# Where the raw weight pieces of a fused attention, Fourier and feed-forward kernel lie, and when the last of them are converted

## The chip, the cores and the metric

The kernel runs on one core of a Trainium2 chip. The core has five engines that run side by side and each take their own instructions strictly in order: TensorE (PE, with its weight loads as PEld), VectorE (DVE), ScalarE (ACT), GpSimd (POOL) and SyncE (SP), which here only issues DMAs. The metric is the device time of one execution in microseconds; lower is better.

## The reference

For 4 sequences of 768 tokens and 8 heads of 64 features, queries and keys are each given to one of 16 clusters, and a query attends only to keys of its own cluster. The heads are laid side by side (512 features), a two-dimensional Fourier transform is taken over tokens and features, its real part is added, and a normalised two-layer feed-forward net follows.

```python
mask = q_assign[:, :, :, None] == k_assign[:, :, None, :]
scores = np.where(mask, scale * np.matmul(q, k.transpose(0, 1, 3, 2)), -1000000000.0)
...
X = np.fft.fft(np.fft.fft(x, axis=1), axis=2)
u = x + np.real(X).astype(np.float32)
...
un = (u - mu) / np.sqrt(var + 1e-06)
ch = np.maximum(un @ w_ch1, 0.0) @ w_ch2
return (u + ch).astype(np.float32)
```

The two weight matrices (512 x 2048 and 2048 x 512) arrive as 64-bit floats. The kernel turns each into a pair of 16-bit matrices (a high and a low half) on the chip.

## The kernel before, in words

**Steps.** `Overlap.run` writes the order of the work out by hand. The attention has 16 pairs of heads, each with 6 blocks of 128 queries; one block of one pair is one step. Step 5 scores the first block, step 100 the last; steps 5 to 28 are pairs 0 to 3, which make up the first sequence. In each step `Attention.scores` runs 16 matmuls (L320, L325), VectorE reduces the two score tiles to their maxima (L339, result `rmx`, kept in `att.late`), ScalarE takes exponentials (L342) and rounds them to 16 bits (L350), GpSimd subtracts to get the low half (L351), and SyncE issues a DMA transpose per head (L353, tile `pt`). Two or three steps later `Attention.attend` multiplies with the values (L371 to L373). `prep` loads and splits the queries and keys of the next pairs (L210, L216, L236). While pairs 0 to 3 are scored, the exponentials lie in the tile `X[1]`, which nothing else needs yet.

**Weights.** `Weights.run` is a generator that is called once per conversion step k, beside the attention. The 2 x 16 pieces of 128 x 512 values are numbered 0 to 31: 0 to 15 are the first layer's, 16 to 31 the second's. `load` fetches a piece raw (512 KB, L481). `signs` (L506, L507, ScalarE, two pieces per instruction) picks the exponent bits of the piece into a sign image; `block` (L491, 8 matmuls per 4 pieces, then L494 and L58 to L61 on VectorE) finds the scale of four pieces; `join` (L515 on PE, L519 on VectorE) makes the 32-bit value in PSUM; `halve` writes the high half (L525, ScalarE) and the low half: an even piece by one VectorE instruction (L531), an odd one by a ScalarE copy and a GpSimd subtraction (L528, L529). `relative` (L563 to L569) closes the conversion with small VectorE instructions.

Raw pieces and sign images lie in the `Arena`, 48192 bytes per partition that later hold the transform's and the feed-forward net's activations. There are eight raw places (`RAW`), so the load of piece p waits until piece p - 8 has been joined. Conversion step i is called at attention step 0.684 i: the first join stands ahead of step 5, the last one behind the scores of step 25.

**What follows.** At step 31 `Fourier.fold` folds the first sequence (L641, L642, halves in L625 and L626, two DMA transposes L648); from step 32 the transform's matmuls (L697, L712) and, from step 36, the feed-forward net's (L842, L873) are interleaved with the attention of the next sequence. Only PE's order is taken as written; on the other engines a scheduler places instructions by its own estimate of when they are ready.

## Time and profile before

| what | value |
|---|---|
| runs | 1043.43 us median of 3 (1041.61 to 1048.4) |
| the profiled execution | 1042.51 us, its span 1040.7 us |
| mean granted PE clock | 0.951 |
| busy in the span | PE 916.0 us, DVE 607.9, ACT 604.3, POOL 588.1 |
| read from HBM | 42.52 MB |

The profile's views used below are: the table of stretches (busy time of each engine between two moments, with the number of instructions, the granted clock and the DMA share, which can pass 1 because it is the packets' time over the time of 16 engines); the groups of instructions by line and shape; the timeline of one engine; and the list of waits (which engine waited at which line for which). A step is timed from its first L339 instruction on VectorE to the next step's.

### The profile page before, as it was taken

To read this page: it belongs to the slowest core of one execution; us is meant where nothing else is said; L and a number is where in the kernel's file an instruction comes from. 1 tells how busy PE (TensorE), PEld (TensorE's weight loads), DVE (VectorE), ACT (ScalarE), POOL (GpSimd) and SP (SyncE) were. 2 spreads that over 40 slices of the span, in tenths; PEclk is the share of its full clock that TensorE was granted. 3 is DMA by queue.
4 is the path that set the end of the run, shared out by engine and by line. 5 is a ranking of instruction groups with operands and counts; after the bars stand their busy time and mean duration, and the time that the engine had idled before them with its cause. 6 is when DMAs were issued, how large, how long until landed. Compare 5 with 4: busy or idle time off the path is not lost.

```text
span 1040.7 us, 23567 instructions
## 1 busy us (share of the span) xinstructions
PE 916.0 (88%) x9396; PEld 592.0 (57%) x9416; DVE 607.9 (58%) x1264; ACT 604.3 (58%) x948; POOL 588.1 (57%) x694
## 2 busy tenths in 40 slices
PE   4776676667999999998999999997999999899998
PEld 2243343444765757554756758555757676586683
DVE  6788789778555555668656555577555423621110
ACT  5899897645755656454756747455666552342230
POOL 2466577556766756636857747448857553362230
PEclk9588978879999999998999999998999999999999
DMA  7799998977668676679667767488656561411000
GB/s 266 197 252 242 276 208 188 180 145 147 146 104 178 104 148 143 121 143 171 114 134 148 139 123 148 92 149 176 115 108 128 96 125 32 81 42 31 11 11 21
DMA packets 396239, 140.01 MB, mean 135 GB/s; under 512 B 381784, under 2 KB 381792, under 8 KB 396128
## 3 DMA queue, kind: packets, MB, share of 16 engines
q1 hardware_dynamic: 396128, 138.50, 65.1%
q8 instruction: 73, 1.20, 0.5%
q14 instruction: 38, 0.31, 0.1%
HBM read 42.52 MB, written 6.29 MB: 47 GB/s over the span
## 4 chain that ended last, share of the span: by engine, by line
PE 43%; DVE 14%; DMA 9%; POOL 9%; ACT 7%; issue 7%; SPq 1%; ACTq 0%; POOLq 0%; DVEq 0%
PE ps_f L873 17%; PE ps_f L842 15%; PE ps_big L320 4%; DMA pt<-ph 4%; POOL ph L351 3%; DVE ps_big L339 3%; ACT ph L350 2%; DMA scr<-in_k_dram 2%; DMA arena<-arena 1%; PE ps_o L371 1%; ACT p L342 1%; PE ps_f L697 1%; PE ps_o L372 1%; PE ps_o L373 1%; DVE X L339 1%
## 5 line engine op out<-in xcount | busy, mean ns | idle before, releaser
L351 POOL TENSOR_TENSOR ph<-p,ph 128x768 f16<-128x768 f32 x144 | 241.8, 1687 | 181.3 <-ACT ph L350 149.0
L842 PE MATMUL ps_f<-arena,w1h 128*128 128x256 f16 x1536 | 271.1, 276 | 22.5 <-ACT arena L851 9.5
L873 PE MATMUL ps_f<-w2h,arena 128*128 128x512 f16 x768 | 239.0, 379 | 0.5 <-ACT arena L851 0.5
L842 PE MATMUL ps_f<-arena,w1l 128*128 128x256 f16 x768 | 211.9, 276 | 0.0
L342 ACT ACTIVATE p<-ps_big,rmx 128x768 f32<-128x768 f32 x144 | 128.9, 900 | 133.8 <-DVE ps_big L339 120.3
L873 PEld LDWEIGHTS <-arena 128*128 128x128 f16 x1152 | 108.7, 98 | 127.2 <-issue 5.8
L842 PEld LDWEIGHTS <-w1h 128*128 128x128 f16 x1536 | 151.9, 99 | 36.7 <-issue 12.7
L852 POOL TENSOR_TENSOR arena<-arena 128x256 f16<-128x256 f32 x192 | 128.6, 680 | 74.5 <-ACT arena L851 70.4
L339 DVE TENSOR_SCALAR_CACHE_REDUCE ps_big<-ps_big,sce 128x768 f32<-128x768 f32 x144 | 141.4, 1020 | 44.2 <-PE ps_big L325 44.2
L320 PE MATMUL ps_big<-hlk,hlq 64*128 64x384 f16 x1152 | 127.7, 346 | 36.2 <-ACT p L342 22.1
L873 PE MATMUL ps_f<-w2l,arena 128*128 128x512 f16 x384 | 145.5, 379 | 0.0
L371 PE MATMUL ps_o<-v,pt 128*128 128x66 f16 x1152 | 121.8, 197 | 14.5 <-DVE X L387 7.4
L851 ACT ACTIVATE arena<-ps_f,wrel 128x256 f16<-128x256 f32 x192 | 90.6, 474 | 70.9 <-DVE arena L848 69.2
L350 ACT CAST ph<-p 128x768 f16<-128x768 f32 x144 | 117.9, 832 | 15.9 <-DMA pt<-ph 15.3
L848 DVE TENSOR_SCALAR arena<-ps_f,wrel 128x256 f32<-128x256 f32 x96 | 46.2, 481 | 136.4 <-POOL arena L852 82.1
L371 PEld LDWEIGHTS <-pt 128*128 128x128 f16 x1152 | 108.6, 99 | 27.6 <-issue 16.8
L372 PE MATMUL ps_o<-v,pt 128*128 128x64 f16 x1152 | 121.7, 197 | 0.0
L373 PE MATMUL ps_o<-v,pt 128*128 128x66 f16 x1152 | 121.2, 196 | 0.0
L372 PEld LDWEIGHTS <-pt 128*128 128x128 f16 x1152 | 109.2, 99 | 2.7
L320 PEld LDWEIGHTS <-hlq 64*128 64x128 f16 x1152 | 55.0, 98 | 96.0 <-issue 64.8
L373 PEld LDWEIGHTS <-pt 128*128 128x128 f16 x1152 | 109.4, 101 | 0.0
L842 PEld LDWEIGHTS <-w1l 128*128 128x128 f16 x768 | 75.9, 99 | 23.3 <-issue 14.2
(176 smaller groups left out, 1328.9 us busy)
## 6 DMA issues: line engine op xcount, KB each, us to landing
arena<-in_moe_w_ch_dram SPq DMA_DIRECT2D x32, 512.0 KB
scr<-in_q_dram SPq DMA_DIRECT2D x16, 384.0 KB
scr<-in_k_dram SPq DMA_DIRECT2D x16, 384.0 KB
vst<-in_v_dram SPq DMA_DIRECT2D x16, 384.0 KB
out_dram<-arena SPq DMA_DIRECT2D x24, 256.0 KB
pt<-ph SPq DMA_TRANSPOSE x168
arena<-in_cs_dram SPq DMA_DIRECT2D x12, 192.0 KB
arena<-in_ss_dram SPq DMA_DIRECT2D x12, 192.0 KB
```

Source lines behind the costliest of these rows:

```text
L320: nc.tensor.matmul(out=ps[j][:, hf, 0:SH], lhsT=hq[rows[j], a, sl], rhs=hk[rows[j], c, hs], start=(i == 0), stop=False)
L339: self.mark = nc.vector.tensor_scalar(out=ju, in0=ps[j][:, :, 0:SH], scalar1=ne, scalar2=None, op0=ALU.mult, op1=ALU.min, accum_out=m)
L342: nc.scalar.activation(x, ju, AF.Exp, bias=m, scale=-1.0)
L350: nc.scalar.copy(out=ph[:, 0], in_=p32)
L351: nc.gpsimd.tensor_tensor(out=ph[:, 1], in0=p32, in1=ph[:, 0], op=ALU.subtract)
L371: nc.tensor.matmul(out=o[:, at:at + W], lhsT=hi, rhs=v16[:, kt, 0:W], start=(kt == 0), stop=False)
L372: nc.tensor.matmul(out=o[:, at:at + D], lhsT=hi, rhs=v16[:, kt, 66:130], start=False, stop=False)
L373: nc.tensor.matmul(out=o[:, at:at + W], lhsT=lo, rhs=v16[:, kt, 0:W], start=False, stop=(kt == ST - 1))
L842: nc.tensor.matmul(out=ps.rearrange("p (t x) -> p t x", x=P), lhsT=a[:, dc, fs], rhs=c[:, :, dc], start=(i == 0), stop=(i == 11))
L851: nc.scalar.activation(hh[:, f], ps, AF.Relu, scale=rel[:, f:f + 1])
L852: nc.gpsimd.tensor_tensor(out=hl[:, f], in0=r, in1=hh[:, f], op=ALU.subtract)
L873: nc.tensor.matmul(out=ps, lhsT=a[:, f, ts], rhs=c[:, f], start=(i == 0), stop=(i == 47))
```

## The change

Three things move. (1) The arena is laid out anew: two of the eight raw places, the small tables `ID`, `TOP`, `MX`, `ONE` and `X32` change their offsets, and the transform's table `CD` starts 32 bytes later. (2) Pieces 8 to 15 are loaded into the space of the second layer's halves (`w2h`, `w2l`), which are written only from piece 16 on, so 16 raw pieces can be held at once. For pieces 8 to 23 GpSimd first copies one column of `att.late` into the raw place (L484), and the load waits for that copy: it can't start before the scores of the step in which it is written. (3) Pieces 24 to 31 get raw places and sign images of their own (`RAWB`, `PNB`), which lie in the first 20.5 KB of the arena and near its end, where the feed-forward net's activations come later, so that they can still be converted while `fold` and the transform use the rest; two images lie in parts of `X` (`spare`).

With these, the conversion's pace changes: from step 8 of the generator on it is called every 0.85 attention steps instead of every 0.684. The loads follow a table (`TIMES`), `signs` is called one place earlier, the signs of pieces 8 to 15 and 24 to 31 take two instructions of 512 values each instead of sharing two of 1024, and the odd pieces from 25 on make their low half on VectorE.

```diff
+    RAW, PN = tuple(4128 * i for i in range(6)) + (28864, 32992), (24768, 39168, 43264)
+    LAST = 24
+    RAWB, PNB = (0, 4104, 8208, 12312), (16416, 18464, 45216)
+    EXTRA, AHEAD, THR = 8, 7, 1
+    TIMES = {8: 1, 9: 1, 10: 2, 11: 3, 12: 4, 13: 4, 14: 5, 15: 6, 16: 7, 17: 8, 18: 10, 19: 11, 20: 13, 21: 14, 22: 16, 23: 17,
+             24: 18, 25: 19, 26: 20, 27: 21, 28: 25, 29: 26, 30: 27, 31: 28}
...
+        self.spare = X[0][:, 2:6, 3 * P:DM].bitcast(BF16), X[1][:, 4:6, DM // 2:DM].bitcast(BF16)
...
     def raw(self, k):
-        n, e = len(self.RAW), self.EXTRA
-        if n <= k < n + e:
-            o = 16 * DM - 2064 * ((k - n) // 2 + 1)
-            return self.w2[k % 2].rearrange("p a x -> p (a x)")[:, o:o + 4 * DM + 8].bitcast(U16)
-        return self.arena.at(self.RAW[(k if k < n else k - e) % n], [P, 4 * DM + 8], U16)
+        n = len(self.RAW)
+        if n <= k < n + self.EXTRA:
+            return self.w2x[k % 2][:, 4 * DM * ((k - n) // 2):][:, 0:4 * DM + 2].bitcast(U16)
+        at = self.RAW[k % n] if k < self.LAST else self.RAWB[(k - self.LAST) % len(self.RAWB)]
+        return self.arena.at(at, [P, 4 * DM + 2], U16)
...
     def load(self, k):
+        if len(self.RAW) <= k < self.LAST and self.att.late is not None and self.THR:
+            self.nc.gpsimd.tensor_copy(out=raw[:, 2:4].bitcast(F32), in_=self.att.late)
...
     def signs(self, k):
+        if k >= self.LAST or n <= k < n + self.EXTRA:
+            for i in range(k, k + 2):
+                if k < self.LAST:
+                    b = at(self.PN[k // 2 % 3], [P, 2, 2, DM], BF16)[:, :, i % 2]
+                else:
+                    b = at(self.PNB[i % 4], [P, 2, DM], BF16) if i % 4 < 3 else self.spare[i // 4 % 2]
+                self.bits[i] = b
+                top = self.raw(i)[:, 4:4 + 4 * DM - 3:4]
+                for j, t in enumerate((top.bitcast(I16), top)):
...
+                    nc.scalar.activation(o, t, AF.Relu, bias=self.off[:, j:j + 1], scale=8.0)
+            return
...
-        if k % 2:
+        if k % 2 and k < self.LAST:
             x = self.arena.at(self.X32, [P, DM], F32)
...
-            if k % 2 == 0 and 0 <= k + 2 < 32:
+            if k == self.LAST + 4:
+                self.signs(k + 2)
+                yield
+            if k == self.LAST + 2:
                 self.signs(k + 2)
...
+            if k % 2 and 0 <= k + 3 < self.LAST + 4:
+                self.signs(k + 3)
...
-    W0, WD = 0, 0.684
+    W0, WD, WE = 0, 0.684, 0.85
...
-        n = 32 + self.wts.AHEAD + 2
+        n = 32 + self.wts.AHEAD + 3
         for i in range(n):
-            at(int(self.W0 + i * self.WD), 6, weights, None)
+            at(int(self.W0 + i * self.WD) if i < 8 else int(T0 + (i - 7.3) * self.WE), 6, weights, None)
```

Joins per stretch of steps, counted from the two built programs: ahead of step 5 one in both; steps 5 to 21, 25 before and 20 now; steps 22 to 28, 6 and 7; steps 29 to 32, none and 4. The block of pieces 28 to 31 and `relative` stand behind step 28 now. From step 32 on PE's order is the same in both. The changed file is 31 lines longer, so its lines bear higher numbers: L519 becomes L544 (join), L531 becomes L556 (low half), L494 becomes L500 (block), L641, L642 and L626 become L671, L672 and L656 (fold), L481 becomes L487 (load).

The first place is VectorE from the maximum of the values of a later pair (L248) through the fold of the first sequence, steps 31 and 32. Before:

```order
L641 TENSOR_TENSOR arena<-X_63 128x1536
L248 TENSOR_REDUCE amx<-vst 128x1
L339 TENSOR_SCALAR ps_big,rmx<-ps_big,sce 128x2x384 x2
L201 SCALAR_TENSOR_TENSOR v_2831<-vst,scp,v_2831 128x6x64
L626 SCALAR_TENSOR_TENSOR arena<-arena,vseq 128x768
L641 TENSOR_TENSOR arena<-X_63 128x1536
L642 TENSOR_TENSOR arena<-arena 128x3x255
L626 SCALAR_TENSOR_TENSOR arena<-arena,vseq 128x768
L339 TENSOR_SCALAR ps_big,rmx<-ps_big,sce 128x2x384 x2
```

The same place in the changed kernel:

```order
L556 SCALAR_TENSOR_TENSOR w2l<-ps_f,wsc,w2h 128x512
L248 TENSOR_REDUCE amx<-vst 128x1
L339 TENSOR_SCALAR ps_big,rmx<-ps_big,sce 128x2x384 x2
L201 SCALAR_TENSOR_TENSOR v_2840<-vst,scp,v_2840 128x6x64
L656 SCALAR_TENSOR_TENSOR arena<-arena,vseq 128x768
L671 TENSOR_TENSOR arena<-X_63 128x1536
L544 SCALAR_TENSOR_TENSOR ps_f<-arena,ps_f 128x512 x2
L672 TENSOR_TENSOR arena<-arena 128x3x255
L556 SCALAR_TENSOR_TENSOR w2l<-ps_f,wsc,w2h 128x512 x2
L339 TENSOR_SCALAR ps_big,rmx<-ps_big,sce 128x2x384 x2
L201 SCALAR_TENSOR_TENSOR v_3014<-vst,scp,v_3014 128x6x64
L656 SCALAR_TENSOR_TENSOR arena<-arena,vseq 128x768
```

Five conversion instructions now stand inside the fold, and the second halving of the fold (L626, now L656) has moved behind the two maxima of step 32 and a value split.

The second place is the DMA queue, SP, from the transposes of step 6 to those of step 8 (`ph` and `p` are the two heads' tiles of one step). Before:

```order
L353 DMA_TRANSPOSE pt<-ph 128x12x128
L353 DMA_TRANSPOSE pt<-p_357 128x12x128
L481 DMA arena<-in_moe_w_ch_dram 128x2048
L353 DMA_TRANSPOSE pt<-ph 128x12x128
L353 DMA_TRANSPOSE pt<-p_411 128x12x128
L481 DMA arena<-in_moe_w_ch_dram 128x2048 x2
L353 DMA_TRANSPOSE pt<-ph 128x12x128
L481 DMA arena<-in_moe_w_ch_dram 128x2048
L353 DMA_TRANSPOSE pt<-p_492 128x12x128
L303 DMA_TRANSPOSE oht<-oh 128x9x128
L481 DMA arena<-in_moe_w_ch_dram 128x2048 x2
```

In the changed kernel:

```order
L353 DMA_TRANSPOSE pt<-ph 128x12x128
L353 DMA_TRANSPOSE pt<-p_362 128x12x128
L487 DMA w2l<-in_moe_w_ch_dram 128x2048
L353 DMA_TRANSPOSE pt<-ph 128x12x128
L353 DMA_TRANSPOSE pt<-p_408 128x12x128
L487 DMA w2h<-in_moe_w_ch_dram 128x2048
L487 DMA w2l<-in_moe_w_ch_dram 128x2048
L487 DMA w2h<-in_moe_w_ch_dram 128x2048
L353 DMA_TRANSPOSE pt<-ph 128x12x128
L353 DMA_TRANSPOSE pt<-p_474 128x12x128
L487 DMA w2l<-in_moe_w_ch_dram 128x2048
L303 DMA_TRANSPOSE oht<-oh 128x9x128
```

The loads of pieces 12, 13 and 14 now stand in a row ahead of the transposes of step 8, where two loads stood.

## The prediction

> **What bounds the kernel now.** I read the page's slices first, then the table of stretches cut at attention steps, then the groups of instructions in these stretches, and last VectorE's timeline where the first sequence is folded.

> ```profile
> span 1040.7 us, 23567 instructions
> PE   4776676667999999998999999997999999899998
> DVE  6788789778555555668656555577555423621110
> ACT  5899897645755656454756747455666552342230
> 260.00:860.00 600.00, 568.82 (x6265) 377.24 (x6264) 352.71 (x728) 355.86 (x574) 378.62 (x435) 0.99 0.70 133
> ```

> A slice is 26 us. From the eleventh on PE is at 9 nearly everywhere, and it is busy for 568.82 of the 600 us from 260 on: there the matmuls set the pace, and whatever comes late before 260 us is handed on to the end. In the first ten slices PE is at 4 to 7, and VectorE and ScalarE at 6 to 9. This first quarter is the part that the change touches. The steps in it are bounded by VectorE's first maximum of each:

> ```profile
> 28.79 1.01 DVE L339 TENSOR_SCALAR_CACHE_REDUCE X<-ps_big,sce 128x768 f32<-128x768 f32 x1
> 145.86 1.02 DVE L339 TENSOR_SCALAR_CACHE_REDUCE X<-ps_big,sce 128x768 f32<-128x768 f32 x1
> 191.54 1.02 DVE L339 TENSOR_SCALAR_CACHE_REDUCE ps_big<-ps_big,sce 128x768 f32<-128x768 f32 x1
> 221.58 1.01 DVE L339 TENSOR_SCALAR_CACHE_REDUCE ps_big<-ps_big,sce 128x768 f32<-128x768 f32 x1
> ```

> These are steps 5, 22, 29 and 32. Cut there, the stretches read (time, PE, PE loads, VectorE, ScalarE, GpSimd busy, then clock, DMA share, GB/s):

> ```profile
> 28.80:145.90 117.10, 83.67 (x932) 45.40 (x947) 97.98 (x202) 107.17 (x139) 71.42 (x63) 0.83 1.06 242
> 145.90:191.50 45.60, 30.96 (x404) 19.43 (x409) 38.42 (x85) 35.90 (x49) 31.32 (x27) 0.81 0.86 173
> 191.50:221.60 30.10, 16.70 (x211) 10.38 (x208) 22.62 (x29) 15.32 (x20) 19.35 (x14) 0.72 0.86 160
> 221.60:258.20 36.60, 28.92 (x329) 18.71 (x327) 28.64 (x67) 21.44 (x35) 20.93 (x23) 0.92 0.78 159
> ```

> Steps 5 to 21 take 6.9 us each with 25 joins among them, steps 22 to 28 take 6.5 us with 6. ScalarE is busy 0.915 of the first stretch and 0.787 of the second; the DMA share falls from 1.06 to 0.86; VectorE alone has the same share in both, 0.837 and 0.843. So the conversion fills ScalarE and the DMA engines early, and VectorE is as full as it gets all along. No single engine is the bound; ScalarE and VectorE feed each other in order.

> **The change part by part.** *Steps 5 to 28* (28.8 to 191.5, 162.7 us). The prices:

> ```profile
> L519 DVE SCALAR_TENSOR_TENSOR ps_f<-arena,ps_f 128x512 uint32<-128x512 uint32 x31 | 21.0, 685 | 0.7 <-ACT ph L350 0.5 <-PE ps_f L515 0.2
> L531 DVE SCALAR_TENSOR_TENSOR w2l<-ps_f,wsc,w2h 128x512 f16<-128x512 f32 x8 | 5.9, 742 | 1.7 <-ACT w2h L525 1.7
> L494 DVE TENSOR_REDUCE arena<-ps_f 128x1 f32<-128x512 f32 x7 | 4.8, 681 | 0.8 <-PE ps_f L491 0.8
> L59 DVE TENSOR_SCALAR ps_f<-ps_f 128x1 int32<-128x1 int32 x7 | 1.1, 161 | 0.1
> L566 DVE TENSOR_SCALAR wrel<-arena 128x16 f32<-128x16 f32 x1 | 0.5, 504 | 0.0
> L506 ACT ACTIVATE arena<-arena 128x1024 int16<-128x1024 int16 x13 | 15.9, 1224 | 4.6 <-PE ps_f L491 3.3 <-DMA arena<-in_moe_w_ch_dram 1.2
> L525 ACT ACTIVATE w2h<-ps_f,wsc 128x512 f16<-128x512 f32 x16 | 10.9, 688 | 1.4 <-DVE ps_f L519 1.4
> L528 ACT ACTIVATE arena<-ps_f,wsc 128x512 f32<-128x512 f32 x16 | 11.0, 685 | 0.0
> L529 POOL TENSOR_TENSOR w2l<-arena,w2h 128x512 f16<-128x512 f32 x4 | 4.6, 1160 | 9.5 <-ACT arena L528 9.5
> ```

> VectorE loses 4 joins (2.74 us), one block (0.68 and four small instructions of about 0.16, together 1.32) and `relative` (0.50 and four small ones, 1.1). Its low halves stay 15: pieces 28 and 30 leave, 25 and one more odd piece come in. That is 5.2 us less: from 97.98 + 38.42 = 136.4 to 131.2 us. At the steady share of 0.838 the stretch would take 156.5 us, a gain of 6.2. ScalarE loses 4 high halves and 4 copies (8 x 0.686 = 5.5). Its sign instructions go from 24 of 1024 values (29.4 us) to 8 of those and 30 of 512. No such short one is in the trace; its price lies between half of 1.22 (0.61) and the 512-value instruction L525 (0.69), so 28.1 to 30.5 us in all. I take the upper end, since L525 is as long and the nearest row: ScalarE goes from 143.07 to about 138.7 us, which at its share over the stretch, 0.879, is 157.7 us, a gain of 5.0. The DMA engines gain nothing here: all pieces from 8 on are still loaded between steps 5 and 28. I take 5.5 us, between the two engines that feed each other. At the one end stands no gain, if the transfers set the pace; at the other 11 us, if the whole stretch ran at ScalarE's early share of 0.915 (138.7 / 0.915 = 151.6).

> *The waits of the loads.* GpSimd gets 16 copies like that which already guards the loads of the values:

> ```profile
> L189 POOL COPY vst<-rmx x14: 177/187/198, 38.6 to 711.2; 128x1 f32<-128x1 f32 x14
> POOL vst L189 <- DVE X L339: 3.7, 1, 3.7
> ```

> They are 3.0 us against the 4 subtractions of 1.16 that it loses, and GpSimd is busy 102.7 of 162.7 us, so I cost them at nothing; without that cover 3.0. Each waits for the second maximum of a step, and behind it on GpSimd stands the subtraction (L351) of that step or the next, for which the transposes wait. That subtraction waits for an exponential and a rounding behind the first maximum anyway, which end later, so the copy is the later of the two only in single places; the one such wait in this stretch took 3.7 us.

> *Steps 29 to 31.* Here nothing was converted, and now four pieces are: on VectorE 4 joins, 4 low halves, a block and `relative`, 2.74 + 2.97 + 1.32 + 1.1 = 8.1 us, in a stretch where it was busy 22.62 of 30.1. Where the rest was:

> ```profile
> 200.96 0.95 DVE L216 TENSOR_REDUCE amx<-scr 128x1 f32<-128x768 f32 x1 [4.51 <-DMA scr<-in_q_dram]
> 203.00 1.02 DVE L339 TENSOR_SCALAR_CACHE_REDUCE ps_big<-ps_big,sce 128x768 f32<-128x768 f32 x1
> 215.28 1.76 DVE L641 TENSOR_TENSOR arena<-X 128x1536 f32<-128x1536 f32 x1
> 217.07 2.27 DVE L642 TENSOR_TENSOR arena<-arena 128x765 f32<-128x765 f32 x1
> 220.35 1.31 DVE L626 SCALAR_TENSOR_TENSOR arena<-arena,vseq 128x768 f16<-128x768 f32 x1 [1.00 <-ACT arena L625]
> 223.45 0.61 DVE L201 SCALAR_TENSOR_TENSOR v<-vst,scp,v 128x384 f16<-128x384 f32 x1
> 218.58 3.64 PE L697 MATMUL ps_f<-arena 128*128 128x257 f16 x18 [0.56 <-DMA arena<-arena]
> 227.69 1.20 PE L697 MATMUL ps_f<-arena 128*128 128x257 f16 x6
> ```

> The one long gap, 4.51 us before step 30, is a wait for a load of queries; the block, the join of piece 28 and `relative` now stand ahead of it or just in it, and can fill it. What is left, 8.1 - 4.5 = 3.6 us, falls into steps 30 and 31, where VectorE runs from 203.00 to 221.58 with little idle: five conversion instructions stand inside the fold. The fold's second halving feeds the even matmuls that began at 227.69, and PE takes everything in order, so I let all 3.6 us through. Bounds: 0.6, if all 7.5 idle us are filled, and 10.6, if none is and the halving also waits for the two maxima and the value split that now stand ahead of it (from 221.58 to 223.45, and 0.61: 2.5).

> [...]

> PE's share of the moved pieces, 16 matmuls, lies in 13 idle us of this stretch. The same matmuls (line L491 alone) in the first stretch:

> ```profile
> 28.80:145.90 117.10, 12.64 (x44) 4.79 (x48) 0.83 1.06 242
> ```

> At 12.64 / 44 = 0.287 us each they would cost 4.6 us uncovered. The small shifts in the arena change no instruction, and from step 32 on PE's order is the same in both: nothing.

> **The sum.** 1042.51 - 5.5 + 3.6 = 1040.6 us for the profiled execution. The median of the runs shown is 0.9 us above that execution; I give 1041.0.

> **The rivals.** *The even pace pays more.* In steps 5 to 21 PE's matmuls for the scores and joins wait for ScalarE and VectorE in many places,

> ```profile
> PE ps_big L320 <- DVE X L339: 13.4, 18, 2.9
> PE ps_f L515 <- ACT arena L528: 4.0, 2, 2.7
> PE ps_o L371 <- DMA pt<-p: 4.8, 5, 2.1
> ```

> and two joins in a row, which hold two of the three PSUM buffers, mostly become one. With the 11 us of the upper end and 2 us lost at the fold: 1042.5 - 11 + 2 = 1033.5. Against it: VectorE's share does not fall when the pieces end, so it isn't ScalarE alone that holds the steps.

> *The fold gets the bill.* If the conversion's instructions and the displaced halving lie wholly in the chain from the fold to the even matmuls, 10.6 us are lost there: 1042.5 - 5.5 + 10.6 = 1047.6, slower than before. It decides from 5.5 us on that reach PE at the even matmuls. For it speaks that they stand in the middle of the fold in VectorE's order; against it the idle 7.5 us and PE's own waits there.

> *The transfers are the pace.* The DMA share over steps 5 to 28 is (1.06 x 117.1 + 0.86 x 45.6) / 162.7 = 1.00, and the same pieces are moved. Then steps 5 to 28 stay as long as they are: 1042.5 + 3.6 = 1046.1. Against it: PE lost only 4.8 us to late transposes `pt<-p`.

> *Loads in a row hold up transposes.* Three loads stand ahead of step 8's transposes on SP; at the stretch's 242 GB/s, 1.57 MB take 6.5 us, and a second such row stands near step 20. If both reach the path: 1042.5 - 1.9 + 13 = 1053.6. A transpose is used three steps, some 20 us, later, and the old kernel had such a row too:

> ```profile
> 133.87 4.55 SPq L481 DMA_DIRECT2D arena<-in_moe_w_ch_dram  x3
> ```

> [...]

> **How the numbers follow.** Chances: my forecast 0.48, the even pace 0.2, the fold 0.16, the transfers 0.12, the row of loads 0.04. The forecast's own range is 1037 to 1045; the 1030 to 1052 that I give takes in the unknown costs and the first three rivals. About 1% (10.4 us) is what a measurement of this kernel can tell from no change. Only the even pace comes under 1033, in a good half of its cases, and the forecast in few: faster 0.17. Slower by over 1% needs the row of loads, or the fold without the relief: 0.12. Same: 0.71.

> **What would show it.** Right: step 5 to step 29 takes 155 to 159 us instead of 162.7, ScalarE's share falls below 0.9 in steps 5 to 21, and step 29 to the even matmuls grows from 36.2 by 2 to 5 us; PE is unchanged behind 260 us. The even pace: step 5 to 29 in 152 or less. The fold: the even matmuls over 42 us behind step 29. The transfers: step 5 to 29 in 161 or more, with a DMA share of 1.0 or more in steps 22 to 28. The loads: waits of PE for `pt` over 10 us. My reading is wrong altogether if the time changes behind 260 us, or if VectorE's share in steps 5 to 28 moves away from 0.84 while they get shorter.

## The result and the profile after

The changed kernel takes 1048.34 us (median of 20 runs, 1041.54 to 1056.13) against 1042.87 us before (20 runs, 1039.36 to 1049.23): ratio 1.0051, 95% interval 1.0032 to 1.0071. It is slower by 0.5%, 5.5 us; the prediction had 1041.0 us, faster by 0.2%. A second measurement, later, gave 1.0060 (1.0030 to 1.0090). The traced execution took 1047.6 us with a span of 1045.3.

The page's head and its slices, as shown of before:

```profile
span 1045.3 us, 23613 instructions
PE   4677676668899899998999999998899999999998
DVE  6778877787547556568747555568555333531110
ACT  5889887754756656646556747455756543352230
```

From the tenth slice on PE is at 8 and 9, where before it was at 9 nearly everywhere from the eleventh. Where the time is lost, the starts of the steps show. The same four first maxima, of steps 5, 22, 29 and 32 (start and duration in us, and in brackets how long VectorE waited and for what):

```profile
29.40 1.01 DVE L339 TENSOR_SCALAR_CACHE_REDUCE X<-ps_big,sce 128x768 f32<-128x768 f32 x1
145.24 1.02 DVE L339 TENSOR_SCALAR_CACHE_REDUCE X<-ps_big,sce 128x768 f32<-128x768 f32 x1 [1.15 <-PE ps_big L325]
193.84 1.03 DVE L339 TENSOR_SCALAR_CACHE_REDUCE ps_big<-ps_big,sce 128x768 f32<-128x768 f32 x1 [2.84 <-PE ps_big L325]
224.52 1.01 DVE L339 TENSOR_SCALAR_CACHE_REDUCE ps_big<-ps_big,sce 128x768 f32<-128x768 f32 x1
```

The stretches between them, in the columns of the prediction's table (time, then busy time of PE, PE loads, VectorE, ScalarE, GpSimd, then clock, DMA share, GB/s):

```profile
29.40:145.20 115.80, 81.28 (x915) 43.38 (x915) 93.71 (x189) 100.27 (x138) 74.29 (x78) 0.82 1.04 235
145.20:193.80 48.60, 32.73 (x415) 18.94 (x414) 37.70 (x82) 40.46 (x58) 29.18 (x25) 0.82 1.00 197
193.80:224.50 30.70, 20.92 (x227) 12.37 (x228) 25.48 (x43) 17.90 (x25) 15.82 (x12) 0.72 0.80 152
224.50:265.80 41.30, 32.42 (x337) 19.70 (x335) 29.45 (x69) 21.66 (x35) 21.37 (x24) 0.83 0.75 142
```

VectorE was relieved as forecast and ScalarE by half of it: over steps 5 to 28 VectorE is busy 131.4 us (136.4 before, 131.2 forecast) and ScalarE 140.7 (143.1, 138.7). The time did not follow: 164.4 us instead of 162.7. VectorE's share fell to 0.799, ScalarE's to 0.856. Steps 5 to 21 got 1.3 us shorter, 22 to 28 3.0 longer, 29 to 31 0.6 longer, 32 to 35 4.7 longer. Behind step 36, which starts at 265.8 instead of 258.2, about 3 us come back up to the end (779.5 us from there, 782.5 before).

**Where the time stands in the trace.** Three places stick out. The first is step 8, which lasts 11.7 us (4.7 before). Rows of VectorE at its end (those between them left out):

```profile
51.67 0.56 DVE L279 TENSOR_TENSOR ac<-ps_f,mx 128x384 f32<-128x384 f32 x1
54.72 0.55 DVE L285 TENSOR_REDUCE mx<-ac 128x24 f32<-128x384 f32 x1 [2.49 <-POOL ac L281]
56.43 2.00 DVE L293 TENSOR_TENSOR oh<-ac,mx 128x96 bf16<-128x96 f32 x2
58.96 1.28 DVE L544 SCALAR_TENSOR_TENSOR ps_f<-arena,ps_f 128x512 uint32<-128x512 uint32 x2
60.81 1.00 DVE L339 TENSOR_SCALAR_CACHE_REDUCE X<-ps_big,sce 128x768 f32<-128x768 f32 x1
```

The cluster choice of the next pair, a block and two joins stand ahead of step 9's maxima, and VectorE waits 2.49 us there for GpSimd's product, ahead of which three of the new copies stand. Before, the same L285 came behind these maxima. But steps 9 and 10 take 10.1 us instead of 15.9: step 11 starts 41.5 us behind step 5, and did 41.3 before. Almost nothing is left of the 7 us.

The second place is step 25, 11.7 us instead of 8.3. PE's matmuls for the scale of pieces 24 to 27:

```profile
165.14 1.46 PE L497 MATMUL ps_f<-arena 128*128 128x512 bf16 x6
172.16 1.01 PE L497 MATMUL ps_f<-X,arena 128*128 128x512 bf16 x2 [5.56 <-DVE X L387]
```

VectorE meanwhile:

```profile
169.39 0.95 DVE L248 TENSOR_REDUCE amx<-vst 128x1 f32<-128x768 f32 x1 [2.72 <-DMA vst<-in_v_dram]
170.39 1.02 DVE L201 SCALAR_TENSOR_TENSOR v<-vst,scp,v 128x384 f16<-128x384 f32 x1
171.55 0.56 DVE L387 TENSOR_TENSOR X<-ps_o,rs 128x384 f32<-128x384 f32 x1
```

The image of piece 27 lies in `X[0]`, token tiles 2 to 5, columns 384 to 511. The division L387 of head pair 2 writes columns 256 to 383 of tiles 3 to 5. They share no byte, but their rows interleave, and the two matmuls that read the image waited 5.56 us for that division, which itself stands on VectorE behind a wait for values. The wait is there again in the second trace of the changed kernel and, further down, in that of experiment 9, which keeps the image in its place:

```profile
PE ps_f L497 <- DVE X L387: 4.8, 1, 4.8
PE ps_f L497 <- DVE X L387: 6.2, 1, 6.2
```

The third place is the fold, step 32, 15.9 us instead of 11.4. VectorE:

```profile
221.87 1.40 DVE L672 TENSOR_TENSOR arena<-arena 128x765 f32<-128x765 f32 x1
223.20 1.40 DVE L556 SCALAR_TENSOR_TENSOR w2l<-ps_f,wsc,w2h 128x512 f16<-128x512 f32 x2
226.92 1.01 DVE L656 SCALAR_TENSOR_TENSOR arena<-arena,vseq 128x768 f16<-128x768 f32 x1
```

TensorE, the even matmuls (L727) and the scores of step 33:

```profile
232.64 1.22 PE L727 MATMUL ps_f<-arena 128*128 128x257 f16 x6 [0.34 <-DMA arena<-arena]
238.22 1.89 PE L320 MATMUL ps_big<-hlk,hlq 64*128 64x384 f16 x12
```

The second halving L656 stands behind the conversion and the two maxima, and the even matmuls start 38.8 us behind step 29 (36.2 before). That is 2.6 us (0.4 in the second trace of the changed kernel, where they start 36.6 behind). Behind them TensorE's clock differs: the scores took 1.15 us before at a granted clock of 1.00, and 1.89 here at 0.59. PE in steps of 3.4 us (time, busy, granted clock, DMA share, GB/s), in this trace and below it in a second trace of the same kernel:

```profile
226.10:229.50 3.40, 1.86 (x36) 1.00 1.29 146
229.50:232.90 3.40, 1.42 (x24) 1.00 1.04 204
232.90:236.30 3.40, 3.40 (x17) 0.51 1.05 200
236.30:239.70 3.40, 3.40 (x19) 0.50 0.35 72
239.70:243.10 3.40, 3.39 (x29) 0.99 0.96 175
```

```profile
225.60:229.00 3.40, 1.27 (x11) 1.00 1.07 151
229.00:232.40 3.40, 3.29 (x44) 0.50 1.05 219
232.40:235.80 3.40, 3.25 (x24) 1.00 1.08 197
```

In all eighteen traces of this case the clock goes down for 3.4 us or a multiple of it (3.41, 6.83 or 10.24 us in the first of the changed kernel). Here it does so behind a stretch in which PE was busy for 1.42 and for 1.27 of 3.40 us. In the first trace the even matmuls and the next scores run through two such stretches at half clock, in the second the attention's matmuls take one and the even ones run at full clock, and step 29 to 36 is 72.0 us in the one and 66.9 in the other (66.7 and 66.8 in the two traces of before). The stretch before need not be idle: 42% of busy time, 1.42 of 3.40 us, was little enough (the last section has the count over all traces).

### The profile page after: what moved, and what is told of

It is laid out like the page before. It is cut to its first block, busy times and chain, and to the rows that moved or that the text cites. A ratio compares the mean times of both kernels' runs of the same rounds, so it can differ in the third digit from the quotient of the medians.

```text
span 1045.3 us, 23613 instructions
## 1 busy us (share of the span) xinstructions
PE 925.2 (89%) x9416; PEld 593.3 (57%) x9416; DVE 608.1 (58%) x1268; ACT 604.5 (58%) x960; POOL 585.4 (56%) x706
## 4 chain that ended last, share of the span: by engine, by line
PE 48%; DVE 14%; DMA 11%; ACT 9%; POOL 9%; issue 7%; SPq 2%; ACTq 0%; POOLq 0%; DVEq 0%
PE ps_f L903 17%; PE ps_f L872 16%; PE ps_big L320 5%; DMA pt<-ph 4%; DVE ps_big L339 4%; POOL ph L351 3%; ACT ph L350 2%; DMA scr<-in_k_dram 2%; DMA vst<-in_v_dram 2%; DMA arena<-arena 2%; PE ps_o L371 2%; PE ps_o L373 1%; PE ps_o L372 1%; PE ps_f L727 1%; PE ps_big L325 1%
## 5 line engine op out<-in xcount | busy, mean ns | idle before, releaser
L351 POOL TENSOR_TENSOR ph<-p,ph 128x768 f16<-128x768 f32 x144 | 240.8, 1679 | 188.2 <-ACT ph L350 154.3
L320 PE MATMUL ps_big<-hlk,hlq 64*128 64x384 f16 x1152 | 131.7, 353 | 44.8 <-DVE X L339 24.2
L339 DVE TENSOR_SCALAR_CACHE_REDUCE ps_big<-ps_big,sce 128x768 f32<-128x768 f32 x144 | 141.5, 1020 | 48.8 <-PE ps_big L325 48.7
L371 PE MATMUL ps_o<-v,pt 128*128 128x66 f16 x1152 | 122.0, 197 | 5.0 <-DVE X L387 3.0
L350 ACT CAST ph<-p 128x768 f16<-128x768 f32 x144 | 117.7, 832 | 14.3 <-DMA pt<-ph 13.5
L371 PEld LDWEIGHTS <-pt 128*128 128x128 f16 x1152 | 109.0, 99 | 17.9 <-issue 12.7
L320 PEld LDWEIGHTS <-hlq 64*128 64x128 f16 x1152 | 56.4, 100 | 109.7 <-issue 72.3
L872 PEld LDWEIGHTS <-w1l 128*128 128x128 f16 x768 | 75.9, 99 | 23.4 <-issue 14.1
```

Of the source, the lines that this page charges most:

```text
L320: nc.tensor.matmul(out=ps[j][:, hf, 0:SH], lhsT=hq[rows[j], a, sl], rhs=hk[rows[j], c, hs], start=(i == 0), stop=False)
L339: self.mark = nc.vector.tensor_scalar(out=ju, in0=ps[j][:, :, 0:SH], scalar1=ne, scalar2=None, op0=ALU.mult, op1=ALU.min, accum_out=m)
L350: nc.scalar.copy(out=ph[:, 0], in_=p32)
L351: nc.gpsimd.tensor_tensor(out=ph[:, 1], in0=p32, in1=ph[:, 0], op=ALU.subtract)
L371: nc.tensor.matmul(out=o[:, at:at + W], lhsT=hi, rhs=v16[:, kt, 0:W], start=(kt == 0), stop=False)
L872: nc.tensor.matmul(out=ps.rearrange("p (t x) -> p t x", x=P), lhsT=a[:, dc, fs], rhs=c[:, :, dc], start=(i == 0), stop=(i == 11))
```

## The experiments

Sixteen more measurements followed. The table has the median, the ratio to the kernel before, measured beside it, with its 95% interval, and from the one trace of each the length of three stretches, between starts of first maxima (L339), in us.

| kernel | median us | ratio (interval) | step 5 to 29 | 29 to 36 | 36 to end |
|---|---|---|---|---|---|
| before, two traces | 1042.87 | | 162.7, 163.3 | 66.7, 66.8 | 782.5, 782.1 |
| changed, two traces | 1048.34, 1049.40 | 1.0051, 1.0060 | 164.4, 166.5 | 72.0, 66.9 | 779.5, 781.9 |
| 1 image moved | 1047.36 | 1.0030 (1.0004-1.0055) | 161.2 | 70.9 | 782.9 |
| 2 loads not held | 1053.91 | 1.0097 (1.0076-1.0118) | 161.8 | 70.5 | 780.8 |
| 3 old pace | 1049.99 | 1.0049 (1.0028-1.0070) | 169.8 | 69.5 | 782.1 |
| 4 half loads | 1046.70 | 1.0030 (1.0008-1.0052) | 164.1 | 70.8 | 779.7 |
| 5 image and fold, two traces | 1042.05, 1043.25 | 0.9965 (0.9945-0.9985), 0.9985 (0.9962-1.0007) | 160.4, 162.8 | 70.8, 70.3 | 779.4, 780.3 |
| 6 before, halving displaced | 1041.20 | 0.9957 (0.9932-0.9982) | 164.4 | 67.4 | 778.5 |
| 7 before, slower pace | 1050.52 | 1.0050 (1.0023-1.0077) | 171.0 | 66.2 | 779.5 |
| 8 as 5, held a step earlier | 1044.72 | 1.0003 (0.9979-1.0027) | 162.8 | 69.8 | 779.8 |
| 9 fold only | 1044.56 | 1.0012 (0.9991-1.0033) | 167.3 | 68.1 | 781.8 |
| 10 as 5, ScalarE less | 1050.19 | 1.0065 (1.0041-1.0089) | 165.3 | 73.5 | 779.0 |
| 11 as 5, VectorE more | 1051.96 | 1.0094 (1.0071-1.0117) | 166.2 | 70.5 | 780.4 |
| 13 as 5, pace 0.84 | 1051.90 | 1.0079 (1.0049-1.0109) | 164.4 | 71.2 | 781.3 |
| 14 as 5, pace 0.86 | 1051.68 | 1.0072 (1.0042-1.0101) | 167.3 | 69.9 | 786.0 |

Number 12 is the second trace of before, 15 and 16 are the second measurements of 5 and of the changed kernel. Two traces of one program differ by 0.6 to 2.4 us in the first stretch and by up to 5.1 in the second, and a median's interval is 2 to 3 us to either side; smaller differences are not read.

**1. The image of piece 27 moved.**

```diff
-        self.spare = X[0][:, 2:6, 3 * P:DM].bitcast(BF16), X[1][:, 4:6, DM // 2:DM].bitcast(BF16)
+        self.spare = arena.at(24768, [P, 2, DM], BF16), X[1][:, 4:6, DM // 2:DM].bitcast(BF16)
```

> The changed kernel, with the image of piece 27 moved out of the attention's output space X[0] into a free place of the arena; nothing else. Theory 'places' (the loss is made at a few places: the block of pieces 24 to 27 that waited 5.56 us for a division into other columns of X[0], and the fold of the first sequence): PE's wait at that block goes from 5.56 us to under 1, step 25 goes from 11.7 us back to about 8, step 29 starts 3 to 5 us earlier (189 to 191 us), and the time is 1043 to 1046 us. Theory 'transfers' (the DMA engines pace steps 5 to 28, so a wait taken away there is refilled by the next one): step 5 to 29 stays at 163 to 165 us and the time within 1.5 us of 1048.3.

The wait is gone; the eight matmuls now run in one:

```profile
164.23 1.89 PE L497 MATMUL ps_f<-arena 128*128 128x512 bf16 x8
```

Step 25 only falls to 10.3 us, since VectorE's maximum of the block still stands behind the wait for the values; step 28 falls from 7.5 to 4.8, because the scores behind it wait at most 0.9 us for the transpose of the next cluster choice, and 2.96 us in the changed kernel:

```profile
193.29 0.51 PE L325 MATMUL ps_big<-oht 32*128 32x384 bf16 x4 [2.96 <-DMA oht<-oh]
```

Step 29 starts at 190.4 instead of 193.8, as 'places' expected; the median of 1047.4 is above its 1043 to 1046 and is what 'transfers' had, so in the time of the whole run little of the gain shows.

The price is best read where the image acts. Up to 170 us VectorE's order is the same in the changed kernel and in this one. Steps 25 to 28 together take 29.1, 29.3 and 30.0 us in the three traces with the image in `X[0]` and the loads as they were (the changed kernel twice, experiment 9), and 26.3, 26.6 and 26.4 in the three that differ from them by its new place (experiments 1, 5 and 15): 3.0 us. Over steps 5 to 28 the same traces have 164.4, 166.5 and 167.3 against 161.2, 160.4 and 162.8, 4.6 us; the other 1.6 us lie ahead of step 25, where the two groups overlap, and are not the image's.

**2. The loads not held.**

```diff
-    EXTRA, AHEAD, THR = 8, 7, 1
+    EXTRA, AHEAD, THR = 8, 7, 0
```

> The changed kernel without the 16 copies on GpSimd that hold the loads of pieces 8 to 23 until a maximum is known; the loads start as soon as their place is free and SP reaches them. Theory 'places': the one long wait of such copies (8.5 us for a maximum, step 8 to 9, with GpSimd's products of the clusters behind it) goes, step 8 falls from 11.7 to 6 us, but steps 9 and 10 take part of it up, so 0 to 3 us faster: 1045 to 1048. Theory 'transfers': earlier loads stand in front of the transposes on SP and crowd them; waits of PE for transposes grow, 1048 to 1052.

Slower, 1053.9, above both theories: step 5 starts only at 38.9 us (29.4 with the copies). SP now issues the eight loads of pieces 8 to 15 between 10.5 and 19.2 us, ahead of the queries and keys of the next pair. From there to step 29 it takes 161.8 us, 2.6 less than in the first trace of the changed kernel, but with loads that had ten us more. So without the copies the start is 9.5 us later, and the run leaves open whether their waits of 8.5 and 4.9 us cost anything later.

**3. The old pace.**

```diff
-        self.spare = X[0][:, 2:6, 3 * P:DM].bitcast(BF16), X[1][:, 4:6, DM // 2:DM].bitcast(BF16)
+        self.spare = arena.at(24768, [P, 2, DM], BF16), arena.at(26816, [P, 2, DM], BF16)
...
-    W0, WD, WE = 0, 0.684, 0.85
+    W0, WD, WE = 0, 0.684, 0.70
```

> The changed kernel at about the old pace (0.70 of a step for each piece in place of 0.85, so the last piece is converted near step 28 and the fold is free of conversions); the images of pieces 27 and 31 lie in free places of the arena, since the early pace would find the attention's space still in use. Theory 'places': the bill of the fold goes (step 29 to 36 back from 72.0 to about 67 us) and the wait at the block of pieces 24 to 27 too, while steps 5 to 28 are as before, 162 to 165 us: 1041 to 1044 us. Theory 'even pace is worth what the forecast said, and the fold took more than it': steps 5 to 28 get 4 to 6 us longer than in the changed kernel (168 to 170), and the time stays at 1046 to 1050.

The second theory's numbers came: 169.8 us, median 1050.0. With no conversion in the fold, step 32 still took 16.7 us. So the conversion in the fold is not needed to make step 32 long. The displaced halving is not ruled out by this run: it stands behind the two maxima here too (at 227.7 us, the maxima at 225.3 and 226.2).

**4. Half of the loads.**

```diff
-        self.nc.sync.dma_start(out=raw[:, 1:1 + 4 * DM], in_=src.bitcast(U16))
+        n = 2 * DM if k >= 16 else 4 * DM
+        self.nc.sync.dma_start(out=raw[:, 1:1 + n], in_=src.bitcast(U16)[:, 0:n])
```

> The changed kernel, with only the first half of the columns of pieces 16 to 31 loaded: the second half of these pieces is left out and what lay in the place before is converted in its stead. 16 x 0.26 MB, 4.2 MB, fewer are moved, some 11% of what the DMA engines move from step 5 to 29; every instruction on the compute engines stays. Theory 'transfers': these steps get shorter with the bytes, by 8 to 18 us, to 146 to 156 us, and the time falls to 1030 to 1040. Theory 'places': less than 3 us, 1045 to 1049, with a DMA share that falls from 1.0 to about 0.9 instead.

```profile
28.60:138.30 109.70, 82.35 (x919) 43.70 (x919) 89.18 (x190) 97.49 (x134) 71.90 (x77) 0.80 1.00 213
138.30:192.70 54.40, 33.64 (x414) 18.58 (x411) 41.04 (x84) 43.12 (x61) 30.84 (x25) 0.83 0.87 168
```

Step 5 to 29 is 164.1 us against 164.4: 4.2 MB less change nothing in the sum, although the DMA share falls to 0.87 in the second part. 'Transfers' as the pace of the whole stretch is out: it had 8 to 18 us for these bytes. The first part is 6 us shorter and the second 6 us longer; the order of the queues had changed with the loads, and the run doesn't tell the bytes from the order within the parts.

**5 and 15. Image moved, and the halving put back ahead of step 32's maxima.**

```diff
+            with self.tc.issue_after(self.gate.ins) if (pr, st) == (4, 3) else contextlib.nullcontext(): self.mark = nc.vector.tensor_scalar( ...
...
-            self.halve(f[:, :, 0:M], h[:, 0], h[:, 1], s)
+            self.att.gate = self.halve(f[:, :, 0:M], h[:, 0], h[:, 1], s)
```

> The kernel with the image of piece 27 in the arena (the first experiment), and VectorE's second halving of the first fold forced back ahead of the two maxima of step 32, where it stood in the kernel before; the conversion's instructions stay in the fold. Theory 'displaced halving' (it alone makes the bill of the fold): from step 31 to step 33 23.4 to 24 us as before the change, instead of 24.7 to 26, step 36 at 258 to 260 us, time 1043 to 1045.5. Theory 'clock' (the bill is TensorE at half clock behind whatever pause of 2 us it makes there, and pieces 30 and 31 in the three PSUM buffers make such a pause anyway): 24.5 to 26 us from step 31 to 33, and the time within 1.5 us of the 1047.4 of the first experiment.

> The kernel with both edits again, for the spread without any change. Theory 'order': steps 5 to 28 within 1.5 us of 160.4 and the median within 1.5 us of 1042.05. Theory 'chips and runs': these steps differ by 2 us or more, and the median by as much, so that nothing follows from the other two.

The medians, 1042.05 and 1043.25, are 6.3 and 6.2 us below the changed kernel's and 0.35% and 0.15% below before: a version at least as quick as the kernel before. Steps 31 and 32 together take 22.7 and 22.2 us, under the expected 23.4 (24.6 in experiment 1). Yet the traces have 70.8 and 70.3 us from step 29 to 36, as many as the first experiment's 70.9: step 29 grew from 13.1 to 15.0 us. So the gain of the fold's order stands in the medians and in steps 31 and 32, but not in the sum of that stretch. Of the spread without any change, 15 leaves half of each theory: the median within 1.2 us, as 'order' had it, and steps 5 to 28 2.4 us apart, as 'chips and runs' had it.

**6. The displaced halving alone, in the kernel before.** The low half of the fold's second part is issued behind the mark of step 32 (`issue_after(att.mark.ins)`, in a call put behind the scores of pair 4, step 3):

```diff
...
+                if (pr, st) == (4, 3): at(t0 + st, 1.2, low, None)
...
```

> The kernel before, with one thing of the change: the second halving of the first fold stands on VectorE behind the two maxima of step 32 instead of ahead of them. Pieces, places and pace are as before. Theory 'displaced halving': the even matmuls start 1 to 3 us later, step 31 to 33 takes 25 to 27 us instead of 23.4, time 1045 to 1047. Theory 'clock and conversion': the halving is ready in time all the same (the even matmuls began 6 us behind it), step 31 to 33 stays within 1 us of 23.4 and the time within 1.5 us of 1043.

Not slower but 0.43% faster. In its trace the halving ends at 224.9 us and the even matmuls start at 231.2 without a wait for its transposes: displaced behind the maxima alone, it is ready in time. Steps 31 and 32 take 24.2 us together (23.4 and 23.6 in the two traces of before), 0.6 to 0.8 more, which the median doesn't show. By itself, in the kernel before, it is not the cause of the loss.

**7. The slower pace alone, in the kernel before.**

```diff
-            at(int(self.W0 + i * self.WD), 6, weights, None)
+            at(int(self.W0 + i * self.WD) if i < 8 else int(T0 + (i - 7.3) * 0.75), 6, weights, None)
```

> The kernel before, in its old places, with nothing changed but the pace from step 5 on: one piece for 0.75 of a step instead of 0.684, so that the last is converted just before the fold. Theory 'pace' (the slower pace is worth something, and the new places cost it again: with the new places and about the old pace steps 5 to 28 took 169.8 us, with the slow pace 161.2): step 5 to 29 falls from 162.7 to 155 to 159 us, the fold keeps its 66.7 us, time 1036 to 1040. Theory 'in-order waits' (the time of these steps is not set by how full ScalarE and VectorE are): 161 to 165 us, time 1041 to 1046; loads that start later in the old places may even add some.

```profile
30.00:148.80 118.80, 79.73 (x917) 45.00 (x932) 91.63 (x193) 101.80 (x132) 67.20 (x59) 0.82 1.00 228
148.80:201.00 52.20, 36.62 (x421) 22.00 (x426) 41.27 (x94) 42.06 (x57) 34.32 (x30) 0.78 0.93 181
```

Both theories missed: 171.0 us. A slower pace with less work in every early step made the steps longer by 8 us. Together with experiment 3: new places at about the old pace cost 7 us in these steps, a slower pace (0.75) in the old places 8, and both together, with the image moved, gain 1.5.

**8. The loads held by a maximum one step earlier.**

```diff
...
-            self.nc.gpsimd.tensor_copy(out=raw[:, 2:4].bitcast(F32), in_=self.att.late)
+            self.nc.gpsimd.tensor_copy(out=raw[:, 2:4].bitcast(F32), in_=self.att.late if self.att.prev is None else self.att.prev)
```

> The kernel of the fold order run, with GpSimd's 16 copies that hold the loads waiting for the second maximum of the step before instead of the newest one, so that they are still held back from the start, but hardly wait on GpSimd. Theory 'GpSimd's queue' (the copies block the subtractions and the products of the clusters behind them; 8.5 and 4.9 us of waits): these waits fall under 2 us, step 8 from 11.7 to under 8 us, step 5 to 29 to 155 to 159 us, time 3 to 5 us under the fold order run. Theory 'passed on': the long step moves to the next place where VectorE and ScalarE wait for each other, and the sum stays within 1.5 us.

Step 8 stays at 11.9 us and step 5 to 29 at 162.8, the time of the second trace without the edit. The test half failed: the copies into the second layer's space still waited 11.8 us (8.3 in experiment 5), those into the arena 0.9 instead of 8.6. Of what the arena's copies waited nothing came back in the sum; what the other ones cost stays open.

**9. The fold's order alone**, the second edit of 5 without the first.

> The changed kernel with only the fold's order put back (the second halving ahead of the maxima of step 32); the image of piece 27 stays in the attention's output space. Theory 'the order of the fold makes most of the loss': 1042 to 1044.5, hardly above the 1042.05 with both edits, and as narrow a spread of runs. Theory 'each its share': the wait for the image adds its 3.4 us again, 1045 to 1047.

1044.56, ratio 1.0012: at the upper end of the first theory, 2.5 and 1.3 us above the two measurements with both edits. Its runs spread from 1041.2 to 1050.5, not narrowly.

With this run the two edits can be read in pairs of kernels that differ by one of them alone. By the ratios to before, putting the halving back is worth 0.39 and 0.48% with the image in `X[0]` (the changed kernel twice against 9) and 0.65 and 0.45% with the image moved (1 against 5 and 15): 4 to 7 us, more than the intervals leave open. Moving the image is worth 0.21 and 0.30%, and 0.47 and 0.27% with the halving back: 2 to 5 us, about what the intervals leave open. In the traces steps 31 and 32 together take 26.0 and 22.7 us in the changed kernel and 22.0 in 9, 24.6 in 1 and 22.7 and 22.2 in 5 and 15. So the fold's order is the larger of the two in the medians; the 2 us or so in these two steps are the part of it that the traces locate.

**10. ScalarE with less work.**

```diff
-            nc.scalar.activation(x, ps, AF.Copy, scale=s)
+            if k == 1: nc.scalar.activation(x, ps, AF.Copy, scale=s)
```

> The kernel with both edits (image in the arena, fold order), without ScalarE's copies of the odd pieces from 3 to 23 to the place that GpSimd subtracts from; GpSimd subtracts from what the copy of piece 1 left there. This leaves 11 copies of 0.69 us out, 7.5 us of ScalarE's work, and the low halves of those pieces are not computed rightly. Theory 'busy share' (the forecast's way of costing): steps 5 to 28 get shorter by 7.5 / 0.87 = 8.6 us, from 160.4 to about 152, time 1033 to 1036. Theory 'in-order waits': less than half of it, 157 to 163 us, time 1039 to 1045.

```profile
29.00:139.70 110.70, 80.51 (x890) 44.36 (x890) 88.16 (x180) 90.08 (x122) 73.41 (x76) 0.78 1.01 224
139.70:194.30 54.60, 36.08 (x453) 21.78 (x452) 41.95 (x94) 43.53 (x61) 29.35 (x25) 0.84 1.00 217
```

(The cut between the two rows is the start of step 21 here, not 22.) ScalarE is busy 133.6 us instead of 139.8, and the stretch takes 165.3 us instead of 160.4 or 162.8. Less work, more time; the median is 8 us higher. Both theories missed, 'busy share' by 13 us.

**11. VectorE with more work.**

```diff
+            for _ in range(1 + (8 <= k < 24)): nc.vector.scalar_tensor_tensor(out=lo, in0=ps, scalar=s, in1=hi, op0=ALU.mult, op1=ALU.subtract)
```

> The kernel with both edits, with the low half of the even pieces 8 to 22 computed twice on VectorE: 8 instructions of 0.74 us more, 5.9 us. Theory 'busy share': steps 5 to 28 get longer by 5.9 / 0.81 = 7.3 us, to about 168, time 1048 to 1050. Theory 'in-order waits': the idle time of VectorE takes most of it, 159 to 164 us, time 1041 to 1046.

166.2 us and a median of 1052: this time near the 168 of 'busy share' (its median of 1048 to 1050 is exceeded), and as much as experiment 10 had with less work. Taken with it, it proves nothing for the load.

**13 and 14. The same work, the pace moved by a hundredth.**

```diff
-    W0, WD, WE = 0, 0.684, 0.85
+    W0, WD, WE = 0, 0.684, 0.84
```

and 0.86 in the second.

> The kernel with both edits (image in the arena, fold order), the pace 0.84 instead of 0.85 of a step: three of the pieces come one step earlier, the work and its sum are the same. Theory 'busy share': steps 5 to 28 as in the run with 0.85, 160 to 161.5 us, time within 1 us of its 1042. Theory 'order': the queues interleave otherwise at some places, and these steps move by 2 to 6 us to either side, the time with them.

> The same with the pace 0.86: four of the pieces come one step later, the work is the same. Theory 'busy share': 159.5 to 161 us for steps 5 to 28, time within 1 us of 1042. Theory 'order': 2 to 6 us to either side.

Both are 8.4 to 9.9 us above the version with 0.85: 1051.9 and 1051.7 against 1042.05 and 1043.25, on the chip of the second of these. In the trace of 0.84, step 24 takes 14.6 us (7.4 and 7.5 at 0.85). PE there:

```profile
160.06 1.03 PE L497 MATMUL ps_f<-arena 128*128 128x512 bf16 x4
165.38 0.38 PE L497 MATMUL ps_f<-arena 128*128 128x512 bf16 x1 [4.29 <-ACT arena L526]
167.94 2.05 PE L320 MATMUL ps_big<-hlk,hlq 64*128 64x384 f16 x12
```

ScalarE:

```profile
160.07 0.92 ACT L235 ACTIVATE hlq<-scr,scp 128x768 f16<-128x768 f32 x1
160.90 0.92 ACT L235 ACTIVATE hlk<-scr,scp 128x768 f16<-128x768 f32 x1
164.59 1.39 ACT L526 ACTIVATE arena<-arena 128x512 int16<-128x512 int16 x2
```

A block that comes one step earlier meets its sign instructions not yet done, since they stand on ScalarE behind the split of queries and keys; PE waits 4.29 us in the middle of the block, and the next step's scores stand behind it. That is a lump of the kind that step 8 shows: an instruction that is ready later than its place in a queue. These edits of the pace put many instructions elsewhere: up to 320 us, 60 and 74 of the 517 instructions of VectorE stand in another order than in experiment 5. The image's and the fold's edits move few: 14 and 5 of 515 from the changed kernel to 1 and to 9.

**12 and 16. Second traces of before and of the changed kernel.**

> The kernel before, unchanged, for a second trace. Theory 'clock': runs of one program differ by whole stretches of 3.4 us in which TensorE gets half its clock; the first 28 steps agree within 1.5 us with the first trace (step 29 at 191.5), and a longer run has more such stretches behind 200 us, each worth up to 1.7 us. Theory 'transfers': the first steps differ by 2 us or more, with other landing times of the loads.

> The changed kernel again, on the chip of the three others. Both edits together were worth 1048.3 - 1042.05 = 6.3 us between calls. Theory 'two places make the loss': 1046.5 to 1050, 5 to 8 us above the run with both edits in this call, with step 5 to 29 at 163 to 168 us and TensorE's mean clock 0.003 or more below. Theory 'chips': less than 3 us between the two.

The second trace of before starts step 5 1.6 us later and keeps that distance within 0.7: 163.3 and 66.8 us for the two stretches. Step 29 is at 193.7 us, outside the 1.5 us that 'clock' allowed, but most of that was there before step 5. Counted in windows of 1 us from 28 to 1040, it has 102 us at half clock and the first one 98; the changed kernel's have 113 and 105. In the second measurement of the changed kernel all three signs of 'two places make the loss' came: 6.2 us above the kernel with both edits, 166.5 us from step 5 to 29, and a mean clock 0.0067 below.

Over the 20 timed runs of the changed kernel span and clock go together (correlation -0.77, 5.3 us of span for 0.01 of clock), which fits half clock making much of the 15 us between its fastest and its slowest run. With both edits they don't (-0.21 and 0.02 over 12 runs each). The mean clock is 0.9433 and 0.9417 in the two measurements of the changed kernel, with both edits 0.9473 and 0.9484, before 0.9462 to 0.9469 beside the experiments. At 5.3 us for 0.01, 2 to 4 of the 6 us between the changed kernel and the version with both edits would be clock; that is an estimate, which carries the slope of one kernel over to another. Where in the run it is lost is not in one trace of each to be seen, and stays open.

## Why the prediction was wrong, point by point

- **The busy times** were right for VectorE (131.2 forecast, 131.4). ScalarE came out 2 us higher, 140.7 instead of 138.7: a sign instruction of 512 values, bounded by 0.61 and 0.69 us, takes 0.76,

```profile
L526 ACT ACTIVATE arena<-arena 128x512 int16<-128x512 int16 x6 | 4.5, 758 | 0.3 <-DMA arena<-in_moe_w_ch_dram 0.3
```

- **The step that failed is the relief: "At the steady share of 0.838 the stretch would take 156.5 us, a gain of 6.2", and with it the term of -5.5.** Measured, steps 5 to 28 got 1.7 us longer in the profiled execution and 3.2 in the second traces. The work left VectorE as forecast, but the time did not follow it: the share fell to 0.799 instead. A share that is the same in two stretches was taken for a limit; the runs speak against it as one, since 6.2 us less on ScalarE (experiment 10) made these steps 4 us longer and a hundredth of pace 3 to 6 longer. In place of the 5.5 they show two numbers. The wait for the image in `X[0]`, which the prediction did not cost at all, takes 3.0 us in steps 25 to 28. With the image elsewhere steps 5 to 28 take 161.5 us on average instead of 163.0: a relief of 1.5, which is not to be told from what the order moves. There VectorE's share is 0.81 to 0.82 (131.3 of 160.4 us in experiment 5): these steps got shorter while the share left 0.84, the sign that the prediction named for a reading that is wrong altogether.
- **The sum's last step** is a slip: 1040.6 plus the 0.9 us by which the median stood above the execution is 1041.5, and 1041.0 was given. It is small beside the 5.5 us that the change costs.
- **The fold** was sized at 3.6 us up to the even matmuls, "2 to 5" in the list of signs; they came 2.6 later in the profiled execution and 0.4 in the second trace. Over the thirteen traces with four joins behind the start of step 29 they start 36.6 to 40.6 us behind step 29 (39.3 on average), over the five without 35.6 to 36.8 (36.2): 3.1 us, so this term and its path were right. All are under the 42 that the rival of the fold needed. The stretch from step 29 to 36 cost 5.3 us in the profiled execution and 0.1 in the second trace. Half clock lay over the even matmuls and the next scores in the one (6.8 us at 0.51 and 0.50) and ahead of the even matmuls in the other (3.4 us at 0.50); how much of the 5.1 us between them that makes was not shown. The bound of 10.6 and the rival built on it named the displaced halving. In the kernel before it costs nothing in the median (experiment 6); in the changed kernel, together with the conversion in the fold, putting it back is worth 4 to 7 us (experiment 9), more than the 2.5 that the bound gave it. That the rival's 1047.6 us lies near the measured 1048.3 is luck: it had 5.5 us gained ahead of the fold and 10.6 lost in it.
- **The waits of the loads**, costed at nothing with 3.0 uncovered: the copies waited 8.5, 4.9 and 2.8 us on GpSimd, five times in all, far more than thought. Steps 9 and 10 took the longest of these up again; without the waits of the arena's copies nothing was gained (experiment 8). The price is not refuted, the size given for the waits (one of 3.7 us as the pattern) was wrong.
- **The transposes** behind rows of loads: PE waited for `pt` 0.6 and 1.2 us where 10 was the sign; right.
- **The transfers' sign appeared** (164.4 us, above 161, with a DMA share of 1.00), and the rival was false: half loads left 164.1. The image's wait and another order also leave the time unchanged at a high share, so the sign didn't separate them.
- **Behind 260 us** nothing was to change: 779.5 and 781.9 us from step 36 on against 782.5 and 782.1. Right.
- **The fold's own instructions on VectorE** were left at their old times in the sum. L672 took 1.40 us instead of 2.27, but the first L671 2.77 instead of 1.76, and with the second L671 (1.76 in both) the three took 5.93 us instead of 5.79, together nearly as forecast. No run shows what stretched or shortened them. The row of the first L671 is

```profile
210.24 2.77 DVE L671 TENSOR_TENSOR arena<-X 128x1536 f32<-128x1536 f32 x1
```

Shown are the wait for the image (it is there in three traces, gone when the image is moved, and worth 3.0 us in steps 25 to 28); that the fold's order is worth 4 to 7 us in the medians, in two pairs of kernels; that with both put right the change is no longer slower than before (0.35 and 0.15% below it, the second not to be told from no change); that the bytes don't set the pace of the whole stretch; and that the halving alone is harmless in the kernel before. Only argued is how the fold's order makes its 4 to 7 us: steps 31 and 32 have some 2 of them, half clock would be the rest, and no run locates it. The two edits don't make every such kernel quick either: 13 and 14 have both, and are as slow as the changed kernel.

## What to carry to other kernels

A share of busy time that doesn't reach 1 is not a pace: before a relief is priced by it, name the instruction whose wait would end earlier, and follow it into the next queue. Where a scheduler writes the order, run the same work with a trifling change of pace first; what that moves (here 8 to 10 us) is no smaller than most edits are worth. Then read an edit's price where it acts, at the wait that it takes away and the few steps around it, and in more than one pair of kernels. And a borrowed place should share no rows with anything that is still written, even where no byte is shared: here that made a wait of 4.8 to 6.2 us.

## What the runs showed of the hardware

```profile
L293 DVE TENSOR_TENSOR oh<-ac,mx 128x96 bf16<-128x96 f32 x8 | 6.4, 845 | 0.0
```

```profile
L293 DVE TENSOR_TENSOR oh<-ac,mx 128x96 bf16<-128x96 f32 x8 | 3.6, 492 | 0.0
```

The eight instructions of 0.74 us that experiment 11 adds left VectorE's busy time in these steps where it was (130.4 against 131.3 us). In these runs an instruction's time is thus not fixed by its shape; what stretches it, no run shows. So a share of busy time says less of the work than the forecast took it to say.
